# One bank operand for each sum, silu from banks, rounding in two parts, and an own place for the second group's weights

**Chip, cores, metric.** One core of one Trainium2 chip. The metric is the device time of one execution in microseconds (us); medians of several executions are given. TensorE is PE in the profile (its weight loads PEld), VectorE DVE, ScalarE ACT, GpSimd POOL. All runs compared here are of the fast state (e7, run once, has none).

## What is computed

```python
def _attn_ref(x, filt_r, filt_i):                 # x: 8 x 3008 x 256, float32
    X = np.fft.rfft(x, axis=1)
    Y = X * (filt_r + 1j * filt_i)[None, :, :]
    return np.fft.irfft(Y, n=x.shape[1], axis=1).astype(np.float32)

def _moe_ref(x, w_gate, w_val, w_out):            # x: 24064 x 256; weights float64, hidden width 1536
    g = x @ w_gate
    silu = g * (1.0 / (1.0 + np.exp(-g)))
    return (silu * (x @ w_val) @ w_out).astype(np.float32)
```

A filter along the sequence by Fourier transform, then a SwiGLU block over all 24064 tokens.

## The kernel before

The program is 96 steps: 8 batches, each of 4 chunks of tokens times 3 groups of hidden units. A bank is a tile in PSUM, the memory in which PE's products land; most other tiles lie in SBUF. In a step PE makes 26 products of polynomial parts: P and Q (into the four banks k0 to k3, "wk" in the profile), A and B (banks "wa") and E (banks "we"), four matmul records each; it projects the previous step's hidden tile (W1 to W7, banks "wA", "wF", "wG", twelve records each) and does pieces of the next batch's transforms (t0 to t4; "pa", "pb", "pc", "pd"). One string sets the order in which all engines' instructions are issued, and every engine works through its own in that order:

```python
SCHEDULE = """
Q0 n1' h0' Q1 S21' f0 P3 o3' f1 t4.3' t0.0 f3 P1 x0' t0.1 P0 x1' Q2 d1 x2' c0 W1 S00' x3' c1 f2
... (cut) ...
W7 t3.1 E23 o7 W2 e01 l23 g1 t3.2 E01 o2 W5 t3.3 l01 h1 t4.0 B12 o5 t4.1 W4 S01 u12 g0 W3 S11 t4.2
o4
""".split()
BY_POOL = ("01", "12", "13", "23")
```

A token with a prime belongs to the step before. The sums between the products, before the change:

```python
elif kind == "f":   # ACT: bank -> SBUF
    pin(act.mul(self.small(...), t[f"k{i}"], -1.0))
elif kind == "c":   # ACT: bank -> its place in the hidden tile h, in SBUF
    pin(act.copy(out=self.place(i, i), in_=t[f"k{i}"]))
elif kind == "s":   # DVE: two SBUF operands -> bank of A, B
    pin(add(v, self.bank(f"a{at}"), t[f"q{i}"], t[f"p{j}"]))
elif kind == "y":   # GpSimd: two SBUF operands, for four of six pairs
    if at in BY_POOL:
        pin(add(nc.gpsimd, self.small(f"y{at}", 3), self.place(i, i), self.place(j, j)))
elif kind == "e":   # bank of E: by ACT from y, or by DVE from two SBUF operands
    ...
elif kind == "l":   # DVE
    pin(sub(v, self.place(j, i), t[f"e{at}"], t[f"m{at}"]))
elif kind == "g":   # ACT: silu of half a hidden tile, 1504 columns
    pin(act.activation(out=h[:, 4:8], in_=h[:, 4:8], func=AF.Silu))
elif kind == "h":   # DVE: its product, 1504 columns
    pin(v.tensor_tensor(out=h[:, 0:4], in0=h[:, 0:4], in1=h[:, 4:8], op=ALU.mult))
elif kind == "S":   # GpSimd: eight sums of h for the projection
    pin(f(nc.gpsimd, h[:, dst], h[:, a], h[:, b]))
```

`combine_sequence` (token n) makes the sums of the transformed data ("y_t") for a new chunk, by DVE before the change. The float64 weights are rounded to float32 on the chip in 36 half tiles (`round_half`, token "r" in a table by step), before step 0 and in steps 0 to 3 of batch 0; the rounded weights of the three groups then take turns in one place.

Of the kernel before, what the change touches and what calls it, by code (L numbers as in the profile page):

```python
# [53 lines left out]
N1, N2 = 47, 64  # L54
# [27 lines left out]

SCHEDULE = """
Q0 n1' h0' Q1 S21' f0 P3 o3' f1 t4.3' t0.0 f3 P1 x0' t0.1 P0 x1' Q2 d1 x2' c0 W1 S00' x3' c1 f2
t0.2 x4' s01 S10' Q3 s13 x5' o1 c3 A01 A13 m01 t1.0 S31' m13 s03 S20' s23 P2 y13 t1.1 B01 t0.3 d2
A03 u01 A23 c2 t1.2 m03 s02 B13 m23 y12 W6 u13 y23 A02 t2.0 e13 o6 e03 m02 S30' E13 t2.1 t1.3 B03
l13 B23 u03 s12 E03 e12 y01 u23 B02 e02 l03 A12 u02 n3 t2.2 E12 m12 E02 t2.3 l12 e23 t3.0 l02 n2
W7 t3.1 E23 o7 W2 e01 l23 g1 t3.2 E01 o2 W5 t3.3 l01 h1 t4.0 B12 o5 t4.1 W4 S01 u12 g0 W3 S11 t4.2
o4
""".split()  # L90
KS = (-1, 0, 1, 2)
BLOCKS = (0, 1, 3, 2)
PAIRS = ((0, 1), (1, 2), (2, 3), (0, 2), (1, 3), (0, 3))
BY_POOL = ("01", "12", "13", "23")
ORDER = [t for t in SCHEDULE if t[0] in "PQABE"]
SLOT = {p: i for i, p in enumerate(ORDER)}
# [38 lines left out]
def kernel(  # L135
# [23 lines left out]
    t2pool = pool("t2", 2)  # L159
    fpool = pool("fp", 2)  # L160
    tbpool = pool("tb", 3)
    apool = pool("ap", 2)
    bpool = pool("bp", 1)
    gpool = pool("gp", 2)
    t4pool = pool("t4", 2)
    ypool = pool("yp", 2)
    dpool = pool("dram", 2, DRAM)
# [8 lines left out]
    wt_f = wt_t.rearrange("p s z f -> p s (z f)")  # L176
    y_t = cpool.tile([128, 3 * len(PAIRS), TQ], FP32)
    w_dram = wdpool.tile([NG, 128, NPR, 2, 128], FP32, name="w_all")
# [59 lines left out]
    START = 6  # L238
    halves = iter(range(len(weights)))

    def load_weights(i, queue=nc.sync, hold=False):
        if i < len(weights):
            p = spool0 if 2 <= i < 4 else rpool
            raws[i] = p.tile([128, 2, 128, 2], U32, name=f"raw_{i}", tag="raw", bufs=2)
            ins = queue.dma_start(out=raws[i], in_=weights[i][0])
            if hold:
                tc.keep_in_program_order(ins)

    def round_next():


        i = next(halves)
        raw, (use, *at) = raws.pop(i), weights[i][1]
        low, high = raw[:, :, :, 0], raw[:, :, :, 1]
        pw = rpool.tile([128, 2, 128], U32, name=f"pw_{i}", tag="pw")
        w = rpool.tile([128, 2, 128], FP32, name=f"w_{i}", tag="w")
# [4 lines left out]

        pin(v.tensor_scalar(out=man, in0=high, scalar1=0xFFFFF, scalar2=None,
                            op0=ALU.bitwise_and))
        pin(nc.scalar.activation(out=w, in_=man, func=AF.Copy, scale=2.0 ** -20, bias=1.0))
        pin(v.tensor_scalar(out=pw, in0=high, scalar1=20, scalar2=0x7FF,
                            op0=ALU.logical_shift_right, op1=ALU.bitwise_and))
        pin(nc.scalar.activation(out=pw, in_=pw, func=AF.Relu, bias=off_t))
        if i + 1 >= START:

            load_weights(i + 1, nc.scalar, True)  # L270
        v.tensor_scalar(out=pw, in0=pw, scalar1=255.0, scalar2=2.0 ** 23,
                        op0=ALU.min, op1=ALU.mult)
        v.scalar_tensor_tensor(out=pw.rearrange(flat), in0=raw.rearrange(flat2)[:, :, 1],
                               scalar=0x80000000, in1=pw.rearrange(flat),
                               op0=ALU.bitwise_and, op1=ALU.bitwise_or)
        v.scalar_tensor_tensor(out=w.rearrange(flat), in0=raw.rearrange(flat2)[:, :, 0],
                               scalar=2.0 ** -52, in1=w.rearrange(flat),
                               op0=ALU.mult, op1=ALU.add)
        e = nc.gpsimd
        pf = pw.bitcast(FP32)  # L280
        if use == "proj":
            j, l = at
            dst = wo_t[:, j]
            pin(e.tensor_tensor(out=dst[:, ts(l, 2), :], in0=w, in1=pf, op=ALU.mult))
            if l:
                b11, b12, b21, b22, t1, t2, t4 = [dst[:, i] for i in range(7)]
                sub(e, t1, b12, b11)
                sub(e, t2, b22, t1)
                sub(e, b12, b22, b12)
                sub(e, t4, b21, t2)  # L290
            return
        _, i, z = at
        x, y, u = w[:, 0], wt_t[:, SLOT[f"Q{i}"], z], wt_t[:, SLOT[f"P{i}"], z]
        pin(e.tensor_tensor(out=y, in0=w[:, 1], in1=pf[:, 1], op=ALU.mult))
        e.tensor_tensor(out=x if KS[i] else u, in0=x, in1=pf[:, 0], op=ALU.mult)
        if KS[i] == -1:
            sub(e, u, x, y)
        elif KS[i]:
            add(e, u, x, y)
            if KS[i] == 2:  # L300
                add(e, u, u, y)

    def combine_weights(i, j):

        d = j - i
        m = wt_f[:, SLOT[f"A{i}{j}"]]
        ui, uj, yi, yj = [wt_f[:, SLOT[f"{p}{q}"]] for p in "PQ" for q in (i, j)]
        if d == 1:
            negated_sum(m, ui, uj)
        else:  # L310
            add(nc.vector, m, ui, uj)
            nc.vector.tensor_scalar(out=m, in0=m, scalar1=-1.0 / d, scalar2=None, op0=ALU.mult)
        sub(nc.vector, wt_f[:, SLOT[f"B{i}{j}"]], yi, m)
        add(nc.gpsimd, wt_f[:, SLOT[f"E{i}{j}"]], yj, m)

    def keep_weights(g, piece):

        a, b = PIECES[piece]
        nc.sync.dma_start(out=w_dram[g, :, a:b], in_=wt_t[:, a:b])
# [7 lines left out]
    hid = {t: "r" for t in ("P0", "Q2", "W1", "Q3", "A01", "A13", "P2", "B01")}  # L327
    hid |= {f"E{i}{j}": [(i, j)] for i, j in ((0, 2), (1, 3), (0, 3), (0, 1), (2, 3))}
    hid["B12"] = [(1, 2), 0, 1, 2, 3]
    few = {t: "r" for t in ("Q0", "Q1", "P3", "P1")}  # L330
    PREPARE = {0: hid | {t: "r" for t in ("A03", "A23", "A02", "B03")}, 1: hid, 2: few, 3: few}
# [17 lines left out]
    class Spectral:  # L349


        def __init__(self, b):
            self.b = b
            self.d1 = dpool.tile([2 * NS, N2, C], FP32, name=f"d1_{b}", tag="d1")
            self.d2 = dpool.tile([2 * NS, N2, C], FP32, name=f"d2_{b}", tag="d2")
# [25 lines left out]
        def load_two(self, u):  # L381
            if u < N_TWO:
                b = self.b
                if b:
                    self.tb[u] = tbpool.tile([128, NV, 2, 128], FP32, name=f"tb_{b}_{u}", tag="tb")
                    self.load(out=self.tb[u], in_=de_dram[:, ts(u, NV)])

                    f = fpool.tile([128, 2, NV, C], FP32, name=f"f_{b}_{u}", tag="f")
# [5 lines left out]
                p2 = spool0 if b == 0 and u % 2 else t2pool  # L394
                self.t2[u] = p2.tile([128, NV, C], FP32, name=f"t2_{b}_{u}", tag="t2", bufs=2)
# [32 lines left out]
        def stage1(self, u):  # L428

            if self.b:  # L430
                for v in (0, 1, 2) if u == 0 else (u + 2,):
                    self.load_x(v)
# [4 lines left out]
                                         start=True, stop=True))  # L437
            yield
# [5 lines left out]
        def stage2a(self, u):  # L444
# [7 lines left out]
            if self.b:  # L452
                ppool, qpool = apool, bpool
            else:
                ppool = apool if u % 3 == 2 else spool0
                qpool = bpool if u % 2 else spool0
            for i in range(NV):
                self.pinned(nc.tensor.matmul(out=ps[:, i, :], lhsT=self.tb[u][:, i, 0, :],  # L458
                                             rhs=t2[:, i, :], start=True, stop=True))
            pt = ppool.tile([128, NV, C], FP32, name=f"p_{self.b}_{u}", tag="p",  # L460
                            bufs=4 if ppool is spool0 else 2)
            qt = qpool.tile([128, NV, C], FP32, name=f"q_{self.b}_{u}", tag="q", bufs=1)
# [18 lines left out]
        def stage2b(self, u):  # L481
# [6 lines left out]
            p3 = spool0 if self.b == 0 and u % 2 else gpool  # L488
            g = p3.tile([128, NV, C], FP32, name=f"g_{self.b}_{u}", tag="g", bufs=2)
# [42 lines left out]
    def combine_sequence(y, d):  # L532

        v = nc.vector
# [9 lines left out]
        for dst, src, f in ((pe, yb[:, 0:n], -d), (pb, yb[:, d:4], d)):  # L544
            pin(v.scalar_tensor_tensor(out=dst, in0=src, scalar=float(f), in1=pa,
                                       op0=ALU.mult, op1=ALU.add))
# [3 lines left out]
    class Group:  # L550


        def __init__(self, b, k, g, y, following):
            self.b, self.k, self.g, self.y, self.following = b, k, g, y, following
            self.name = f"{b}_{k}_{g}"
            self.tiles = {}
# [4 lines left out]
        def place(self, i, t):  # L561
            at = ((0, 1), (3, 2))[i % 2][t // 2]
            return self.hs[i // 2].rearrange("p (z e) n -> p z e n", z=2)[:, :, at, ts(t % 2, TQ)]

        def small(self, key, bufs):
            t = npool.tile([128, 2, TQ], FP32, name=f"{key}_{self.name}",
                           tag=key if bufs == 1 else key[0], bufs=bufs)
            self.tiles[key] = t
            return t
# [7 lines left out]
        def product(self, p, key, start):  # L577
# [5 lines left out]
            for z in range(2):  # L583
                pin(nc.tensor.matmul(out=ps[:, z], lhsT=wt_t[:, SLOT[p], z], rhs=rhs,  # L584
                                     start=start and z == 0, stop=True, skip_group_check=True))

        def step(self, op):
# [3 lines left out]
            t, v, act = self.tiles, nc.vector, nc.scalar  # L591
            if kind in "PQ":
# [4 lines left out]
            elif kind == "f":  # L597
                pin(act.mul(self.small(f"{'p' if i == 3 else 'q'}{i}", 1), t[f"k{i}"], -1.0))  # L598
            elif kind == "d":
                pin(negated_sum(self.small(f"p{i}", 1), t[f"k{i}"], t[f"q{i}"]))  # L600
            elif kind == "c":
                pin(act.copy(out=self.place(i, i), in_=t[f"k{i}"]))  # L602
            elif kind == "s":
                pin(add(v, self.bank(f"a{at}"), t[f"q{i}"], t[f"p{j}"]))
            elif kind in "AB":
                self.product(op, f"a{at}", False)
            elif kind == "m":
                pin(act.copy(out=self.small(f"m{at}", 5), in_=t[f"a{at}"]))  # L608
            elif kind == "u":
                pin(act.copy(out=self.place(i, j), in_=t[f"a{at}"]))  # L610
            elif kind == "y":
                if at in BY_POOL:
# [231 lines left out]
```

## Time and profile before

| | before |
|---|---|
| time, median of 3 (range) | 3233.56 us (3229.16 to 3238.31) |
| profiled execution | 3229.1 us |
| mean granted clock of PE | 0.969 |
| startup to step 0 | 111.5 us |
| steps 0 to 3 of batch 0 (weights are rounded) | 230.6 us |
| rest of batch 0 | 252.2 us |
| batches 1 to 6 | 2277.6 us |
| batch 7, and the end | 357.2 us |

Read it so: the stretches are differences of step starts; how these are found, the prediction says. 119 us of the 230.6 in the first four steps are standstill or half clock (three steps of 30.3 us, and 21 for step 0, which has no output products yet, would be 112), against some 20 us in each later batch.

### The profile page before, as it was taken

The page shows a single profiled execution, that of the slowest core. Times are in us where ns is not written, and L with a number is a line of the kernel's source. Part 1 is how long each engine was busy: PE and PEld are TensorE (multiplying, and loading weights), DVE is VectorE, ACT ScalarE, POOL GpSimd, SP SyncE. Part 2 cuts the span into 40 slices and gives each one's busy share as a digit, 9 for nine tenths or more (in the row PEclk, how much of TensorE's full clock was granted, in tenths as well). Part 3 has the DMA queues.
Part 4 walks back from the last instruction along what each step waited for, and adds up shares of the span by engine and source line. Part 5 has one row for each costly group of instructions (what it writes and reads, how often), then busy time and mean ns, then how long its engine had stood idle before and what let it go on. Part 6 is the DMA issues. An engine that isn't in the chain of part 4 may idle for free.

```text
span 3229.1 us, 54700 instructions
## 1 busy us (share of the span) xinstructions
PE 2994.4 (93%) x20124; PEld 2849.8 (88%) x20124; DVE 2223.4 (69%) x3198; ACT 1568.9 (49%) x3002; POOL 1558.8 (48%) x1586
## 2 busy tenths in 40 slices
PE   5448999999999999999999999999999999999997
PEld 2347999999998999999999999989989999999997
DVE  5467677667765687656776677766876567767775
ACT  1144544555454544455445555545444554455553
POOL 2255555435454464445453454534544454545555
PEclk9678999999999999999999999999999999999999
DMA  8434656456555565456554566556655555544442
GB/s 228 129 110 161 203 170 185 152 186 208 176 162 163 189 211 167 143 181 197 175 185 156 186 193 191 167 158 193 212 170 158 183 185 187 181 147 143 143 132 68
DMA packets 210483, 551.57 MB, mean 171 GB/s; under 512 B 32502, under 2 KB 105462, under 8 KB 209362
## 3 DMA queue, kind: packets, MB, share of 16 engines
q1 hardware_dynamic: 151116, 462.59, 45.4%
q10 hardware_dynamic: 48864, 57.69, 6.3%
q0 software_dynamic: 10240, 27.80, 2.6%
q8 instruction: 162, 2.65, 0.3%
q14 instruction: 101, 0.83, 0.1%
HBM read 462.76 MB, written 85.20 MB: 170 GB/s over the span
## 4 chain that ended last, share of the span: by engine, by line
PE 79%; DVE 11%; DMA 5%; issue 2%; POOL 2%; ACT 1%; SPq 1%; ACTq 0%; POOLq 0%; DVEq 0%
PE wa L584 22%; PE wA L657 13%; PE wk L584 11%; PE we L584 11%; PE wG L657 7%; DVE wa L199 5%; PE wF L657 4%; PE pd L506 3%; PE pa L436 3%; PE pc L486 2%; PE pb L458 2%; DMA x<-in_x_dram 1%; DMA f<-in_filt_r_dram 1%; DVE h L628 1%; DMA wt_t<-w_all 1%
## 5 line engine op out<-in xcount | busy, mean ns | idle before, releaser
L584 PE MATMUL wa<-y_t,wt_t 128*128 128x188 f32 x4608 | 858.7, 329 | 111.1 <-DVE wa L199 84.1
L584 PEld LDWEIGHTS wa<-y_t,wt_t 128*128 128x128 f32 x4608 | 757.5, 193 | 144.7 <-issue 72.5
L199 POOL TENSOR_TENSOR h<-h 128x376 f32<-128x376 f32 x192 | 190.9, 994 | 1017.6 <-DVE h L628 1017.1
L202 POOL TENSOR_TENSOR h<-h 128x376 f32<-128x376 f32 x576 | 614.5, 1086 | 13.8
L584 PE MATMUL wk<-y,wt_t 128*128 128x188 f32 x3072 | 573.2, 331 | 31.7 <-ACT q L598 21.6
L199 DVE TENSOR_TENSOR wa<-q,p 128x376 f32<-128x376 f32 x576 | 581.7, 1042 | 11.9
L657 PE MATMUL wA<-wo_t,h 128*128 128x128 f32 x4608 | 580.7, 276 | 5.3 <-DVE h L628 3.4
L657 PEld LDWEIGHTS wA<-wo_t,h 128*128 128x128 f32 x4608 | 564.8, 192 | 20.2 <-issue 13.2
L584 PEld LDWEIGHTS wk<-y,wt_t 128*128 128x128 f32 x3072 | 510.5, 196 | 69.8 <-ACT q L598 27.8
L202 DVE TENSOR_TENSOR h<-we,m 128x376 f32<-128x376 f32 x576 | 315.1, 548 | 303.1 <-PE we L584 298.9
L610 ACT COPY h<-wa 128x376 f32<-128x376 f32 x576 | 274.3, 477 | 374.6 <-PE wa L584 353.5
L584 PE MATMUL we<-y_t,wt_t 128*128 128x188 f32 x2304 | 450.0, 325 | 3.5 <-ACT we L616 2.6
L584 PEld LDWEIGHTS we<-y_t,wt_t 128*128 128x128 f32 x2304 | 376.1, 192 | 17.7 <-issue 10.9
L628 DVE TENSOR_TENSOR h<-h 128x1504 f32<-128x1504 f32 x192 | 340.9, 1776 | 69.3 <-ACT h L625 52.3
L608 ACT COPY m<-wa 128x376 f32<-128x376 f32 x576 | 269.0, 477 | 177.0 <-PE wa L584 173.3
L625 ACT ACTIVATE h<-h 128x1504 f32<-128x1504 f32 x192 | 279.8, 1458 | 141.0 <-DVE h L202 137.7
L199 POOL TENSOR_TENSOR y<-h,h 128x376 f32<-128x376 f32 x192 | 218.9, 1140 | 236.6 <-ACT h L602 236.5
L199 DVE TENSOR_TENSOR o<-o,wA 128x384 f32<-128x384 f32 x256 | 141.2, 551 | 232.6 <-PE wA L657 230.1
L657 PE MATMUL wG<-wo_t,h 128*128 128x128 f32 x2304 | 288.5, 275 | 0.2 <-DVE o L199 0.2
L657 PEld LDWEIGHTS wG<-wo_t,h 128*128 128x128 f32 x2304 | 277.1, 192 | 0.3 <-issue 0.3
L602 ACT COPY h<-wk 128x376 f32<-128x376 f32 x384 | 176.2, 474 | 200.2 <-PE wk L584 159.5
L199 POOL TENSOR_TENSOR p<-p,q 128x512 f32<-128x512 f32 x96 | 153.2, 1596 | 172.2 <-DVE q L477 152.0
(77 smaller groups left out, 3115.9 us busy)
## 6 DMA issues: line engine op xcount, KB each, us to landing
wt_t<-w_all SPq DMA_DIRECT2D x186, 896.0 KB
wt_t<-w_all SPq DMA_DIRECT2D x186, 768.0 KB
t<-d SPq DMA_DIRECT2D x192, 128.0 KB
d<-g ACTq DMA_DIRECT2D x192, 128.0 KB
t<-d SPq DMA_DIRECT2D x64, 384.0 KB
d<-t ACTq DMA_DIRECT2D x112, 192.0 KB
tb<-de_tbl SPq DMA_DIRECT2D x84, 256.0 KB
f<-in_filt_r_dram SPq DMA_DIRECT2D x336, 64.0 KB
```

The source lines that it names most:

```text
L199: return eng.tensor_tensor(out=dst, in0=a, in1=b, op=ALU.add)
L202: return eng.tensor_tensor(out=dst, in0=a, in1=b, op=ALU.subtract)
L436: self.pinned(nc.tensor.matmul(out=ps[0:NK], lhsT=wf_t, rhs=self.x.pop(u), start=True, stop=True))
L458: self.pinned(nc.tensor.matmul(out=ps[:, i, :], lhsT=self.tb[u][:, i, 0, :], rhs=t2[:, i, :], start=True, stop=True))
L506: self.pinned(nc.tensor.matmul(out=psv[:, n, :], lhsT=self.t4[k, i][:, n, ts(cb, 128)], rhs=wi_t, start=True, stop=True))
L584: pin(nc.tensor.matmul(out=ps[:, z], lhsT=wt_t[:, SLOT[p], z], rhs=rhs, start=start and z == 0, stop=True, skip_group_check=True))
L602: pin(act.copy(out=self.place(i, i), in_=t[f"k{i}"]))
L608: pin(act.copy(out=self.small(f"m{at}", 5), in_=t[f"a{at}"]))
L610: pin(act.copy(out=self.place(i, j), in_=t[f"a{at}"]))
L625: pin(act.activation(out=h[:, 4:8], in_=h[:, 4:8], func=AF.Silu))
L628: pin(v.tensor_tensor(out=h[:, 0:4], in0=h[:, 0:4], in1=h[:, 4:8], op=ALU.mult))
L657: pin(nc.tensor.matmul(out=self.tiles[at][:, t, :], lhsT=self.hs[i][:, HID[p], t0:t0 + 128], rhs=wo_t[:, JB * q + i, WO[p], :], start=star ...
```

## The change

Its intent, as its code shows it: DVE's sums take one operand from the bank instead of two from SBUF; silu and its product read banks directly, in 16 pieces of 188 columns; the sums over the sequence go to GpSimd (with ACT's multiplications); rounding a half tile is cut in two, and the first part of half i+1 is issued before the second of half i; the second group's weights get a place of their own in step 1 ("lent", later used for transform buffers); x of the next batch is loaded two steps early; and the order is new throughout. The core of the diff (cut: the buffers, the loads, the tables):

```diff
 SCHEDULE = """
-Q0 n1' h0' Q1 S21' f0 P3 o3' f1 t4.3' t0.0 f3 P1 x0' ...
+P3 x1.o' h23' g03' v12' Q0 x2.o' h03' Q2 x3.o' f0 x4.o' t0.0 x03 f2 x5.o' S01' x23 Q1 t0.1 P0 f1
+P2 S00' c0 W1 s13 g0 t0.2 D01 c2 S11' y02 g2 h0 P1 o1 S10' Q3 c1 y01 A13 g1 x01 g3 S21' h1 e01
+t1.0 y12 m13 s01 E01 S20' t1.1 A01 D02 W6 m01 t1.2 D12 l01 B13 u01 o6 B01 v01 g13 W7 S31' h13 g01
+... (cut) ...
+            elif kind == "D":
+                pin(sub(nc.gpsimd, self.small(f"D{at}", "D", 2), t[f"f{i}"], t[f"f{j}"]))
+            elif kind == "x" or kind == "s" and at not in VIA_SBUF[0]:
+                dst = self.small(f"x{at}", "x", 3) if kind == "x" else self.bank(f"a{at}")
+                pin(v.scalar_tensor_tensor(
+                    out=dst, in0=t[f"k{j}"], scalar=-1.0, in1=t[f"f{i}" if j == 3 else f"D{at}"],
+                    op0=ALU.mult, op1=ALU.add))
             elif kind == "s":
-                pin(add(v, self.bank(f"a{at}"), t[f"q{i}"], t[f"p{j}"]))
+                pin(act.copy(out=self.bank(f"a{at}"), in_=t[f"x{at}"]))
+            elif kind == "y" or kind == "e" and at not in VIA_SBUF[1]:
+                dst = self.small(f"y{at}", "y", 2) if kind == "y" else self.bank(f"e{at}")
+                pin(negated_sum(dst, t[f"k{j}"], t[f"c{i}"]))
+            elif kind == "e":
+                pin(act.copy(out=self.bank(f"e{at}"), in_=t[f"y{at}"]))
             elif kind == "l":
-                pin(sub(v, self.place(j, i), t[f"e{at}"], t[f"m{at}"]))
+                pin(sub(v, t[f"e{at}"], t[f"e{at}"], t[f"m{at}"]))
+            elif kind in "gu":
+                ps = t[f"k{i}" if diagonal else f"{'a' if kind == 'g' else 'e'}{at}"]
+                pin(act.activation(out=self.small(op, "g", 3, 1)[:, 0], in_=ps[:, 1], func=AF.Silu))
+            elif kind in "hv":
+                ...
+                pin(v.tensor_tensor(out=dst, in0=ps[:, 0], in1=g, op=ALU.mult))
     def combine_sequence(y, d):
-        v = nc.vector
+        v = nc.gpsimd
         ...
-            pin(v.scalar_tensor_tensor(out=dst, in0=src, scalar=float(f), in1=pa,
-                                       op0=ALU.mult, op1=ALU.add))
+            pin(nc.scalar.mul(dst, src, float(f)))
+            pin(add(v, dst, dst, pa))
+    def weights_of(b, k, g):
+        return wt_1 if (b, k, g) == (0, 0, 1) else wt_t
+        for h in halves[i:i + 1] + (halves[i - 1:i] if i else []):
+            next(h, None)
+                if b + 2 < B and (step, op) == (9, "B01"):
+                    for u in range(3):
+                        following.load_x(u)
```

## The prediction

> **What bounds the kernel now.** I read the page's busy shares first, then the table of stretches, the timeline around one stall, and the waits.
>
> ```profile
> PE 2994.4 (93%) x20124; PEld 2849.8 (88%) x20124; DVE 2223.4 (69%) x3198; ACT 1568.9 (49%) x3002; POOL 1558.8 (48%) x1586
> ...
> PEclk9678999999999999999999999999999999999999
> ```
>
> PE is busy nearly all the time; the rest have room on average. So gain can only come from the stretches where PE stands still. The program is 96 steps (8 batches x 4 chunks x 3 weight groups), each opening with the four banks wk, 32 matmul records; counting those in the timeline gives the step starts, from which I cut the stretches. Columns: busy us of PE, PEld, DVE, ACT, POOL, then granted clock, DMA share, GB/s.
>
> ```profile
> 111.50:200.10 88.60, 36.52 (x128) 29.29 (x128) 55.45 (x135) 26.26 (x61) 36.31 (x64) 0.61 0.40 134
> 200.10:261.50 61.40, 38.32 (x212) 34.13 (x211) 43.41 (x81) 27.21 (x56) 32.07 (x45) 0.78 0.40 134
> 261.50:301.00 39.50, 33.16 (x200) 30.27 (x199) 27.60 (x51) 19.76 (x40) 19.56 (x24) 0.91 0.48 151
> ...
> 1042.80:1073.10 30.30, 30.30 (x201) 27.75 (x200) 19.09 (x32) 16.74 (x32) 12.55 (x13) 1.00 0.66 205
> 1196.80:1233.30 36.50, 32.53 (x227) 31.98 (x226) 25.72 (x28) 18.12 (x34) 16.77 (x20) 0.95 0.46 152
> 1263.50:1298.10 34.60, 32.24 (x211) 30.78 (x210) 26.48 (x38) 15.42 (x29) 16.49 (x17) 0.95 0.56 178
> ```
>
> The first three are steps 0 to 2 of batch 0; step 3 takes 41.1 us. The last three are steps 2, 7 and 9 of batch 2. Step 2 is what a step without a stall looks like. In the chain a product (4 records) takes 0.64 us, an output product (12 records) 1.34, a spectral piece 0.86: 26 x 0.64 + 7 x 1.34 + 5 x 0.86 = 30.3 us, just the 30.30 seen. Batch 2's twelve steps take 38.3, 31.4, 30.2, 30.2, 31.2, 31.4, 31.0, 36.5, 30.3, 34.6, 29.6, 27.7; the same sum for their own pieces is 358, so the batch loses 24 us, mostly in steps 0, 7 and 9. Batches 1 to 6 all repeat this (18 to 24 us lost). A stall in step 7 of batch 5, on DVE, PE and POOL:
>
> ```profile
> 2346.66 5.54 DVE L199 TENSOR_TENSOR wa<-q,p 128x376 f32<-128x376 f32 x1
> ...
> 2352.35 0.88 PE L584 MATMUL wa<-y_t,wt_t 128*128 128x188 f32 x4 [2.52 <-DVE wa L199]
> ...
> 2348.01 0.98 POOL L199 TENSOR_TENSOR y<-h,h 128x376 f32<-128x376 f32 x1
> 2348.95 0.97 POOL L199 TENSOR_TENSOR y<-h 128x376 f32<-128x376 f32 x1
> 2349.89 0.96 POOL L202 TENSOR_TENSOR h<-h 128x376 f32<-128x376 f32 x1
> 2350.82 0.96 POOL L199 TENSOR_TENSOR y<-h 128x376 f32<-128x376 f32 x1
> ```
>
> One DVE sum of two SBUF tiles takes 5.54 us, and ends just after POOL's run of back-to-back adds; PE waits 2.5 us for it, and the clock falls after (0.95 over the step). That is no accident of one step (min/median/max ns):
>
> ```profile
> L199 DVE TENSOR_TENSOR wa<-q,p x576: 542/842/5546, 151.9 to 3189.8; 128x376 f32<-128x376 f32 x192
> ```
>
> The waits from step 4 on (total us, times, longest):
>
> ```profile
> PE wa L584 <- DVE wa L199: 39.2, 37, 2.5
> ...
> ACT h L602 <- DVE p L206: 34.8, 51, 2.2
> ...
> PE pa L436 <- DMA x<-in_x_dram: 25.7, 6, 5.0
> ```
>
> At its shortest the sum takes 0.54, on average 1.04 (582 us / 576): 0.5 x 576 = 288 us of DVE's 2223 are waiting inside the instruction. The last line is step 0's stall: the next batch's first x load is issued where it is needed.
>
> **What the Trainium skill says.** "SBUF — State Buffer", Who interferes with whom: a DVE instruction with two SBUF inputs contends with a GpSimd instruction that reads SBUF, the later one blocks in full, and one SBUF input does not contend. The trace agrees: 5.54 against 0.54 us, while sums with one bank operand (o with wA) keep to 0.54 to 0.56. "PSUM — Partial Sum Buffer", PSUM bank collisions raise a hardware error: two engines may not touch a bank at once, reads included. The program orders them: ACT's copy of wk waits for DVE's read of wk (34.8 us above) though it needs nothing from it. This matters for the change, whose banks have more readers. "TensorE: Matmul & The Clock Gate", Part 1: an idle window of some 3.4 us halves the clock; the 0.61 and 0.95 above agree, so a stall costs more than itself. "ScalarE: Activation LUTs", What ACT_TABLE_LOAD costs: 186 + 0.833 N ns for an activation with constants, 499 at 376 elements; the trace has 485 to 495.
>
> **The change part by part.**
> 1. Sums. Every steady DVE sum now has one bank operand (k) and one SBUF operand (f, c or a difference D made by POOL). Per step DVE has 12 such sums, 6 subtractions in place, and 16 products of half width instead of two of 1504 columns (1.78 us each). Durations: 0.55 for 376 columns; the slope from 376 (0.548) to 512 (0.685) is 1 ns a column, so 0.36 for 188. 18 x 0.55 + 16 x 0.36 + output sums 3.1 + spectral 2.3 (both unchanged: their rows over 96) = 21 us a step, against 23 now. The sums over the sequence (1.9 us a step) move to POOL.
> 2. ACT: 16 silus of 188 columns (0.477 less 188 x 0.8 ns = 0.33) instead of two of 1.46; 6 sums and e banks arrive by ACT copies from SBUF; fewer f and c copies: 5.3 + 2.9 (m) + 2.9 (f, c) + 3.0 + 0.6 + 1.9 + 0.6 = 17 us, as now.
> 3. POOL: 8 sums of h (0.98 each unblocked) + 3 D + 3.1 for the sequence + 2.3 = 16.2 us, as now. Nothing passes 21 of 30 us, so PE stays the bound: matmuls are the same in number and size.
> 4. What PE waits for in a steady step. I laid the new order of PE out at the paces above and put the chains beside it. The tightest: P1 ends at 6.66 us of the step; copy c1 (starts 0.2 later, 0.48), sum y01 (0.55), silu g1 (0.33), g3 (0.2 more), copy e01 (0.49) give 9.0 for E01, due at 8.8; A01 comes 0.35 late. The other sums have 0.5 to 3 us of slack, and at most 7 of 7 banks are held (around 23.5 us). I take 0.5 us lost a step, 6 a batch.
> 5. x of the next batch is asked for two steps ahead: step 0's 4 to 5 us go (within the 6 above).
> 6. Rounding. 36 half tiles at 2.05 us of DVE each (0.46 + 0.38 + 0.29 + 0.42 + 0.49). Now in-place weights of the next group wait for PE's last use, and each half crosses DVE, ACT, DVE in turn. In the new kernel the second group has its own place and DVE starts half i+1 before ending half i. DVE then sets step 0: 12 x 2.05 + 6 pairs x 1.7 + 15.5 for the step's own = 50; with waits for the raw loads 60. Step 1: 8 x 2.05 + 10 + 22 = 49, say 51. Steps 2 and 3: four halves ahead of the first sum, 8 us less some 4 of slack, 35 each. Startup to step 0: five halves move ahead of it, mostly under the reload of the transformed data: 112, unchanged.
>
> **Sum.** Startup 112; steps 0 to 3: 60 + 51 + 35 + 35 = 181 (231 now); rest of batch 0: 238 + 5 = 243 (252 now); batches 1 to 6: 6 x (358 + 6) = 2184 (2278 now); batch 7 and end 350 (357 now): 3070, and 4 for time over span: 3074 us, 4.9% faster.
>
> **Rivals.** (a) A new wait takes the old one's place: banks live longer (k3 from 0 to 21 us of a step) and pass DVE, ACT, DVE in turn, and POOL's D is now in the chain, so every step may lose 1.5 us instead of 0.5: +90, 3165. For: more crossings of 0.05 to 0.2 us each; against: slack counted above. (b) Rounding in steps 0 and 1 is bound by raw loads and by the two-input instructions it still has, not by order: nothing gained there, +50, 3124. The chain shows raw loads of 3 to 7 us in step 0, which speaks for it. (c) PE loses almost nothing after step 3 (as in steps 2 and 8 now, 0.1 us): -37, and some faster start: 3030. (d) DVE becomes the bound: its 34 sums and products would each have to be 0.25 us longer than estimated to make 21 into 29.5 us a step; the measured 0.55 of such sums speaks against it, and the time would then be as in (a).
>
> **Range and chances.** (c) is the low end, 3030; half of (a) with part of (b) the high end, 3135. Slower than 3169 (2%) needs (a) in full and more. Faster 0.94, same 0.05, slower 0.01.
>
> **What would show it.** Right: no DVE instruction of the steady part over 0.8 us; DVE busy about 2100; the wait of PE for DVE sums gone; no pa wait for x; steps of 30.2 to 31; batches 1 to 6 near 364 us each; granted clock over 0.98; step 0 near 60. Wrong: step lengths of 32 with PE waiting for ACT copies or for banks, or first steps as long as now.

## The result, and the profile after

The changed kernel takes 3138.43 us (median of 4 runs, 3135.62 to 3141.20), the kernel before in the same job 3234.50: ratio 0.9704, 95% interval 0.9687 to 0.9721, 3.0% faster. (A ratio here is the mean time of one kernel's fast runs over that of the other's of the same rounds, so not quite the ratio of the medians quoted.) The direction was predicted; the time lies 64 us above the predicted one and 3 above the range.

The page's lines of the kernel after, to be held against those of before that the prediction shows:

```profile
PE 2989.7 (95%) x20124; PEld 2831.6 (90%) x20124; DVE 1974.2 (63%) x4446; ACT 1513.4 (48%) x3898; POOL 1585.3 (50%) x1778
...
PEclk9778999999999999999999999999999999999998
```

DVE has 1248 instructions more and 249 us less busy time. The same stretches of the kernel after (steps 0 to 3 of batch 0, then steps 2, 7 and 9 of batch 2; columns as in the prediction):

```profile
115.10:181.20 66.10, 34.57 (x128) 30.47 (x128) 40.67 (x113) 24.69 (x59) 36.86 (x53) 0.68 0.49 168
181.20:235.20 54.00, 39.87 (x212) 36.64 (x211) 42.08 (x103) 24.32 (x63) 29.29 (x46) 0.81 0.26 81
235.20:275.40 40.20, 33.81 (x200) 30.70 (x199) 23.05 (x60) 19.20 (x50) 21.99 (x28) 0.87 0.64 218
275.40:313.70 38.30, 32.89 (x200) 29.78 (x199) 25.53 (x60) 17.89 (x48) 21.38 (x30) 0.91 0.41 132
989.90:1020.60 30.70, 30.70 (x200) 27.69 (x199) 17.80 (x42) 16.05 (x42) 15.81 (x16) 1.00 0.63 201
1145.00:1175.90 30.90, 30.72 (x226) 30.30 (x225) 19.12 (x44) 16.08 (x42) 14.11 (x17) 1.00 0.52 167
1206.90:1239.20 32.30, 31.17 (x210) 29.61 (x209) 23.22 (x50) 14.17 (x37) 18.04 (x20) 1.00 0.64 198
```

Step 7 has gone from 36.5 to 30.9 us at a full clock, and the first four steps from 88.6, 61.4, 39.5 and 41.0 to 66.1, 54.0, 40.2 and 38.3. Two of DVE's groups of sums in the kernel after (min/median/max ns, first and last start):

```profile
L218 DVE SCALAR_TENSOR_TENSOR y<-wk,c x288: 532/549/552, 138.7 to 3088.8; 128x376 f32<-128x376 f32 x144
...
L625 DVE SCALAR_TENSOR_TENSOR x<-wk,f x192: 540/549/552, 121.3 to 3083.2; 128x376 f32<-128x376 f32 x192
```

Where the sum of before ran from 542 to 5546 ns, these never pass 552. Of PE's own waits, from step 4 to the last step (total us, times, longest), these are the two largest; five more rows add up to 2.5 us. The waits for DVE's sums into banks and for x are gone:

```profile
PE we L603 <- ACT we L634: 20.1, 38, 1.5
PE wa L603 <- ACT wa L629: 3.0, 4, 1.1
```

Where the 90 us came from, by stretch:

| us | before | predicted | after |
|---|---|---|---|
| startup to step 0 | 111.5 | 112 | 115.1 |
| steps 0 to 3 | 230.6 | 181 | 198.6 |
| rest of batch 0 | 252.2 | 243 | 246.5 |
| batches 1 to 6 | 2277.6 | 2184 | 2212.7 |
| batch 7 and the end | 357.2 | 350 | 366.5 |
| span | 3229.1 | 3070 | 3139.4 |

And the mean length of each step over batches 1 to 6 (the last row is an experiment below):

| step | 0 | 1 | 2 | 3 | 4 | 5 | 6 | 7 | 8 | 9 | 10 | 11 |
|---|---|---|---|---|---|---|---|---|---|---|---|---|
| before | 36.98 | 31.39 | 30.24 | 30.24 | 31.13 | 31.30 | 30.96 | 35.21 | 30.25 | 34.44 | 29.73 | 27.72 |
| after | 30.68 | 30.64 | 30.61 | 30.61 | 30.71 | 31.67 | 30.97 | 30.97 | 30.96 | 31.81 | 31.09 | 28.08 |
| e10_two_sbuf | 30.95 | 30.91 | 30.88 | 30.88 | 35.64 | 32.05 | 32.25 | 35.40 | 32.13 | 32.29 | 36.36 | 28.43 |

Of the 65 us won in batches 1 to 6, step 0 gave 38 and steps 7 and 9 gave 41, while the other nine steps lost 14.

### The profile page after: what moved, and what is told of

It reads as the page before. It is cut to its first block, busy times and chain, and to the rows that moved or that the text cites. A ratio compares the mean times of both kernels' runs of the same rounds, so it can differ in the third digit from the quotient of the medians.

```text
span 3139.4 us, 57065 instructions
## 1 busy us (share of the span) xinstructions
PE 2989.7 (95%) x20124; PEld 2831.6 (90%) x20124; DVE 1974.2 (63%) x4446; ACT 1513.4 (48%) x3898; POOL 1585.3 (50%) x1778
## 4 chain that ended last, share of the span: by engine, by line
PE 80%; ACT 5%; DVE 3%; POOL 2%; issue 1%; DMA 1%; ACTq 1%; POOLq 0%; DVEq 0%
PE wa L603 21%; PE wA L679 14%; PE wk L603 13%; PE we L603 11%; PE wG L679 8%; PE wF L679 4%; PE pd L525 3%; PE pa L453 3%; PE pc L504 2%; PE pb L479 2%; DVE y L218 1%; ACT g L645 1%; ACT c L622 1%; ACTq L513 1%; DMA out_dram<-o 1%
## 5 line engine op out<-in xcount | busy, mean ns | idle before, releaser
L214 POOL TENSOR_TENSOR h<-h 128x376 f32<-128x376 f32 x576 | 552.5, 984 | 0.0
L214 DVE TENSOR_TENSOR we<-we,m 128x376 f32<-128x376 f32 x576 | 311.3, 556 | 375.8 <-ACT m L638 177.1
L211 POOL TENSOR_TENSOR h<-h 128x376 f32<-128x376 f32 x192 | 185.0, 987 | 430.2 <-DVE h L650 429.7
L645 ACT ACTIVATE g<-wa 128x188 f32<-128x188 f32 x576 | 188.6, 328 | 425.6 <-PE wa L603 267.4
L214 POOL TENSOR_TENSOR D<-f,f 128x376 f32<-128x376 f32 x288 | 280.3, 987 | 72.2 <-ACT f L618 72.1
L645 ACT ACTIVATE u<-we 128x188 f32<-128x188 f32 x576 | 185.0, 326 | 247.6 <-DVE we L214 239.2
L211 POOL TENSOR_TENSOR lent<-lent 128x512 f32<-128x512 f32 (+2 forms) x94 | 116.2, 1237 | 326.3 <-DVE lent L495 304.8
L668 POOL DMA_DIRECT2D out_dram<-o x192 | 110.8, 582 | 315.5 <-DVE o L211 313.4
L650 DVE TENSOR_TENSOR h<-wa,g 128x188 f32<-128x188 f32 x576 | 201.6, 350 | 83.9 <-ACT g L645 79.0
L650 DVE TENSOR_TENSOR h<-we,u 128x188 f32<-128x188 f32 x576 | 201.7, 350 | 78.2 <-ACT u L645 68.3
L218 DVE SCALAR_TENSOR_TENSOR y<-wk,c 128x376 f32<-128x376 f32 x288 | 157.2, 546 | 99.6 <-ACT c L622 98.3
```

What stands on the lines that cost most here:

```text
L211: return eng.tensor_tensor(out=dst, in0=a, in1=b, op=ALU.add)
L214: return eng.tensor_tensor(out=dst, in0=a, in1=b, op=ALU.subtract)
L218: return nc.vector.scalar_tensor_tensor(out=dst, in0=a, scalar=-1.0, in1=b, op0=ALU.mult, op1=ALU.subtract)
L645: pin(act.activation(out=self.small(op, "g", 3, 1)[:, 0], in_=ps[:, 1], func=AF.Silu))
L650: pin(v.tensor_tensor(out=dst, in0=ps[:, 0], in1=g, op=ALU.mult))
L668: pin(nc.gpsimd.dma_start(out=rows[(TOK[t] + skip) // NH:(TOK[t] + 128) // NH, ts(2 * k + i, NH), :], in_=outs[b, k][i][skip:128, t, :]))
```

## The experiments

The theory going in: (1) what steps 7 and 9 gained is the one-bank operand, since a DVE sum of two SBUF operands stands still beside GpSimd; (2) step 0's gain is the early x; (3) the first steps gained by interleaved rounding and by the second group's own place; (4) what the prediction lacks lies in E01's chain and in GpSimd's queue in step 0. The rival: the new order itself does it all. Ratios are set against the kernel before of the same job; the changed kernel's own is 0.9704. Differences in us are between medians of different jobs, in which the kernel before took 3234 to 3238, so a few us of the whole time say nothing by themselves; the step lengths say more.

| run | us | ratio, 95% interval | batches 1 to 6 | steps 0 to 3 |
|---|---|---|---|---|
| changed kernel | 3138.43 | 0.9704 (0.9687 to 0.9721) | 2212.7 | 198.6 |
| e1_w6_first | 3176.24 | 0.9817 (0.9801 to 0.9833) | 2241.8 | 203.1 |
| e2_seq0_dve | 3133.22 | 0.9686 (0.9668 to 0.9703) | 2210.6 | 192.9 |
| e3_seq_dve | 3174.40 | 0.9813 (0.9789 to 0.9837) | 2236.2 | 196.4 |
| e4_x_late | 3195.46 | 0.9879 (0.9863 to 0.9895) | 2268.4 | 198.2 |
| e5_round_whole | 3134.70 | 0.9688 (0.9660 to 0.9717) | 2211.3 | 197.4 |
| e6_before_less_pool | 3232.27 | 0.9994 (0.9969 to 1.0018) | 2280.8 | 225.9 |
| e8_in_place | 3139.40 | 0.9696 (0.9677 to 0.9716) | 2210.1 | 197.6 |
| e10_two_sbuf | 3302.81 | 1.0205 (1.0176 to 1.0234) | 2329.0 | 202.3 |
| e11_proj_early | 3129.66 | 0.9668 (0.9636 to 0.9700) | 2209.6 | 187.2 |
| e12_w6_o6 | 3151.62 | 0.9736 (0.9708 to 0.9765) | 2220.3 | 201.2 |
| e13_best | 3119.22 | 0.9646 (0.9631 to 0.9662) | 2209.1 | 183.3 |

(e7_lock_alone was one look, not timed.)

### Two SBUF operands again, in place (e10_two_sbuf)

Six of the twelve sums of a step have a partner whose copy already lies in SBUF. They read it there instead of in the bank; nothing else changes.

```diff
-  out=dst, in0=t[f"k{j}"], scalar=-1.0, in1=t[f"f{i}" if j == 3 else f"D{at}"],
+  out=dst, in0=t[f"k{j}" if j == 3 else f"c{j}"], scalar=-1.0, in1=...
-  pin(negated_sum(dst, t[f"k{j}"], t[f"c{i}"]))
+  pin(negated_sum(dst, t[f"k{j}" if j == 3 else f"c{j}"], t[f"c{i}"]))
```

> The changed kernel with one thing undone: the six sums whose partner already has a copy in SBUF (01, 02, 12 of each sort) read that copy instead of the bank, so that both operands are in SBUF. Same instructions, same count, same order, same numbers. Theory (an addition by VectorE with two SBUF operands stands still while GpSimd adds, which is why bank operands help): these six groups, now 0.55 us at any time, get a mean of 0.7 to 1.1 us and a longest of over 2 us; TensorE waits more for the sums; batches 1 to 6 take 20 to 60 us more, some 3160 to 3200 in all. Rival (what helps is the new order and the early x; operands do not matter as sums have slack): durations stretch but the time stays within 8 us of 3138.

Measured: 3302.81 us, 2% slower than the kernel before, so the whole gain and more is lost by the operands alone. The same group of sums now, in the same view as above:

```profile
L218 DVE SCALAR_TENSOR_TENSOR y<-c,c x288: 533/1056/7284, 139.5 to 3250.5; 128x376 f32<-128x376 f32 x144
```

One instance in the timeline, step 10 of batch 2, on DVE, POOL and PE:

```profile
1301.24 0.98 POOL L214 TENSOR_TENSOR D<-f,f 128x376 f32<-128x376 f32 x1
1301.76 5.55 DVE L218 SCALAR_TENSOR_TENSOR y<-c,c 128x376 f32<-128x376 f32 x1 [0.40 <-ACT c L622]
1302.18 3.79 POOL L214 TENSOR_TENSOR h<-h 128x376 f32<-128x376 f32 x4
1305.94 0.97 POOL L214 TENSOR_TENSOR D<-f,f 128x376 f32<-128x376 f32 x1
...
1308.59 0.68 PE L603 MATMUL we<-y_t,wt_t 128*128 128x188 f32 x1 [4.25 <-ACT we L635]
```

The same place of the changed kernel:

```profile
1245.50 0.55 DVE L218 SCALAR_TENSOR_TENSOR y<-wk,c 128x376 f32<-128x376 f32 x1 [0.40 <-ACT c L622]
...
1245.93 3.80 POOL L214 TENSOR_TENSOR h<-h 128x376 f32<-128x376 f32 x4
```

The sum with a bank operand takes 0.55 us in the middle of GpSimd's run, the one with two SBUF operands 5.55: it starts during the first of six additions and ends 0.4 us after the last. The product E01 behind it then waits 4.25. Theory 1 holds for step 7, which is back at 35.4 us (the table above; the stall is at E01 now); its size was even underestimated (+116 us in batches 1 to 6 where 20 to 60 were expected), and the rival that operands don't matter falls. Step 9 doesn't come back: 32.3 us here, 31.8 in the changed kernel, 34.4 before. There the sum that PE waited 2.15 us for had begun late, behind over 8 us of DVE work without a pause (sums over the sequence, the product of 1504 columns, the transform); which part of the change removed that is not shown.

### The lock by itself (e7_lock_alone)

Appended to the changed kernel, after all its work: eight DVE sums of two SBUF operands alone, eight beside a run of GpSimd sums, and eight of one bank and one SBUF operand beside such a run.

```diff
+    for n in range(8):                            # alone, then beside the run of GpSimd's
+        pin(add(v, b1, two(0), two(1)))
+    for n in range(12):
+        pin(add(e, dst[2 + n % 2], two(2), two(3)))
+    ...
+    for n in range(8):                            # one operand from a bank
+        pin(add(v, b1, b0, two(1)))
```

> The changed kernel with a measurement of 30 to 40 us after its last step (its time means nothing): eight DVE sums of two SBUF tiles (128x376) into a bank alone; the same eight beside twelve back-to-back adds of POOL; then eight DVE sums of a bank and an SBUF tile beside twelve adds of POOL. Theory of the lock: alone 0.42 to 0.55 us each; beside POOL the two-SBUF sums wait for POOL's whole instruction each time or for the whole run (1 us and more each, one of them perhaps 5 or more); with one bank operand 0.55 us each, as alone. Rival: all three at 0.55.

Measured (timeline of the end):

```profile
3128.47 4.69 DVE L211 TENSOR_TENSOR wmb<-y_t 128x376 f32<-128x376 f32 x8
...
3134.77 14.62 POOL L211 TENSOR_TENSOR lent<-y_t 128x376 f32<-128x376 f32 x13
...
3135.42 9.41 DVE L211 TENSOR_TENSOR wmb<-y_t 128x376 f32<-128x376 f32 x8
...
3150.98 11.26 POOL L211 TENSOR_TENSOR lent<-y_t 128x376 f32<-128x376 f32 x12
3151.52 4.69 DVE L211 TENSOR_TENSOR wmb<-wmb,y_t 128x376 f32<-128x376 f32 x8
```

Alone 4.69 us, beside GpSimd 9.41, and with a bank operand 4.69 again. GpSimd pays too: 14.62 / 13 = 1.12 us for one addition instead of 11.26 / 12 = 0.94. Here the two take turns, at most 1.2 us for a DVE sum. Inside the kernels most of the stretched sums are held up by one or two additions as well; only 6 of 576 in the kernel before (all in step 7) and 25 of the 288 shown of e10 (in steps 4, 7 and 10, and one in step 1) take over 3 us, as they wait for a whole run. What makes it the one or the other isn't settled.

### Less of GpSimd in the kernel before (e6_before_less_pool)

```diff
-BY_POOL = ("01", "12", "13", "23")
+BY_POOL = ()
```

> The kernel before with four sums a step (y) taken from POOL and made by DVE straight into the bank, as it already did for two: POOL has 4.5 us less a step, DVE 4 two-operand sums of 0.55 to 0.65 us more. Theory of the lock: the sums wa get shorter although DVE has more to do, mean from 1.04 to 0.8 us or less and longest from 5.5 to below 4, and the stalls of PE in steps 7 and 9 shrink; time 3180 to 3225. Rival (DVE's load makes the stalls): the sums keep their mean and the time rises above 3240.

Measured: no difference, where 3180 to 3225 us was expected. The longest sum fell from 5.5 to 3.6 us as expected, but the mean only from 1.04 to 0.975, for GpSimd's eight sums of h a step stay (six of them 1.13 us on average), and DVE got the four differences of two SBUF operands in return. Step 7 won 2.9 us (35.21 to 32.33), steps 5 and 9 lost 1.7 and 1.0. This run didn't remove the cause and tells nothing against it; it shows that taking a quarter of GpSimd's busy time away (1559 to 1168 us) was not enough.

### Sums over the sequence on DVE (e3_seq_dve, e2_seq0_dve)

All of them, or only those of the very first chunk, go back to DVE with two SBUF operands.

```diff
-    def combine_sequence(y, d):
-        v = nc.gpsimd
+    def combine_sequence(y, d, on_dve=True):      # e2: False, and True in the one call ahead of step 0
+        v = nc.vector if on_dve else nc.gpsimd
 ... (cut: where on_dve, a multiplication and its sum are one DVE instruction again)
```

> The changed kernel with all sums over the sequence (nine instructions in three steps, both operands in SBUF) back on DVE. Theory of the lock: beside POOL's runs of adds these DVE instructions take far longer than alone (0.55 to 1.3 us for 376 to 564 columns where POOL is idle; up to several us, mean above 1.5 times that), and what DVE holds up behind them gives PE stalls of over 1 us again in steps 0, 3, 6, 9 (after the sums); steps lengthen by 1 to 3 us each, 20 to 60 us over the whole. Rival (load only: DVE has room for 1.9 us a step more, POOL gets rid of 3.1): the DVE instructions keep their lengths and the time stays within 8 us of 3138.

Measured: 36 us more. In step 6 of batch 2, where the run shows most:

```profile
1136.91 2.22 DVE L211 TENSOR_TENSOR y_t<-y 128x188 f32<-128x188 f32 x1
...
1140.31 1.68 PE L607 MATMUL wa<-y_t,wt_t 128*128 128x188 f32 x8 [1.80 <-DVE wa L629]
```

A sum of 188 columns that takes 0.34 us at its shortest in this run took 2.22, and the sum behind it came 1.8 us late for PE: step 6 is 2.1 us longer on average (33.09 against 30.97), and 12.7 of the 23.5 us of batches 1 to 6 are that step. So moving these sums to GpSimd paid in this order, and the stretched sum says for the same reason.

> The changed kernel, but the first chunk's sums over the sequence, before step 0, are made by DVE as in the kernel before; all later ones stay on POOL. Theory: in step 0 PE's wait of 13.5 us comes from these nine operations on POOL (8.8 us), behind which POOL's products of the weight rounding queue; the rounding's two buffers are not free, and DVE and ACT, in program order, stand behind them. Then this wait falls below 4 us, and the time by about 10 us: 3128. Rival (raw weight loads bound step 0): the wait only moves to the loads and the time stays at 3138 within 3.

Measured: 5 us less, half of what was expected. The intervals of the two ratios overlap, but step 0 shows it: 61.8 us, against 66.0 to 66.1 in the changed kernel, e1, e4, e11 and e12, which leave it alone. PE's wait of 13.5 us there became 8.0 (below 4 was expected), as GpSimd's nine sums no longer stood ahead of the rounding. Startup, 117.0 us, is within the 115.1 to 118.0 of those runs.

### Early x undone (e4_x_late)

```diff
-                if b + 2 < B and (step, op) == (9, "B01"):
-                    for u in range(3):
-                        following.load_x(u)
+            if self.b and u == 0:                 # in stage1, where it is needed
+                for v in range(3):
+                    self.load_x(v)
```

> The changed kernel with the early loads of the next batch's first three x pieces undone: they are issued in stage one of step 0, as in the kernel before. Theory: PE's wait for x of 4 to 5 us returns in step 0 of batches 0 to 6, with about 1.7 us of half clock after it: 7 times 5 to 6.5, so 35 to 45 us more, about 3178, and this is half of what batches 1 to 6 gained. Rival (the loads come early enough either way since SP's queue is no longer held): within 10 us of 3138.

Measured: 57 us more, all of it in step 0 of batches 1 to 6: 40.16 us on average instead of 30.68. The wait of PE, from step 0 of batch 1 on: 

```profile
PE pa L456 <- DMA x<-in_x_dram: 40.7, 6, 6.9
```

6.8 us a batch by itself, and the rest of the 9.5 by the halved clock after it. Why it is longer than in the kernel before (4 to 5 us) was not looked into. Theory 2 holds: this smallest part of the diff is worth 56 us in these batches once the rest is there.

### The two parts for rounding (e5_round_whole, e8_in_place)

```diff
-        for h in halves[i:i + 1] + (halves[i - 1:i] if i else []):
+        for h in halves[i:i + 1] * 2:             # e5: a half is ended before the next is begun
```

> The changed kernel with the rounding in one piece again: both parts of half i follow one another, nothing of half i+1 is between them. Theory of the prediction (the parts interleaved save DVE the way over ACT and back, 0.9 us or more for each of 24 to 28 halves): steps 0 to 3 get 15 to 25 us longer in all, about 3158. Rival (the rounding is held by POOL's products, the raw loads and the place of the calls): within 6 us.

```diff
-        return wt_1 if (b, k, g) == (0, 0, 1) else wt_t
+        return wt_t                               # e8: no own place; each half prepared after
+                                                  # PE's last use of what it overwrites
```

> The changed kernel without the own place for the second group's weights: groups 1 and 2 are both prepared in the place of the group in use, each half and each pair put after the last product that uses the old values (so the preparation starts after Q3 and its pairs end with the step). Theory of the prediction: waiting for the old weights' last use was a large part of the first two steps' cost; step 0 and 1 get 10 to 20 us longer together and step 1 and 2 begin with waits for the last pairs: about 3155. Rival (the order of the queues and the raw loads set these steps, not the place): within 5 us of 3138.

Measured: 3134.70 and 3139.40 us, both within 4 us of the changed kernel. Neither part taken away by itself costs anything, so theory 3 has no support. What made the first four steps 32 us shorter then isn't isolated: the order of the weights and of their sums, three raw buffers instead of two, and the fixed places in each engine's order are left, or each of the two parts makes up for the other. Both at once were not undone.

### Projection weights earlier (e11_proj_early)

In the changed kernel PE's first output product of step 2 waits, and again in step 3 (5.0 us):

```profile
246.57 2.50 PE L679 MATMUL wA<-wo_t,h 128*128 128x128 f32 x10 [6.39 <-POOL wo_t L290]
```

The four halves of these weights are rounded at the head of the very step that needs them. In the experiment a step's worth of room is given:

```diff
-   1: eight | pairs,
-   2: {t: "r" for t in ("P3", "Q1", "P0", "P2")},
-   3: {t: "r" for t in ("P3", "Q1", "P0", "P2")}}
+   1: eight | pairs | {t: "r" for t in ("A01", "E02", "W3", "B23")},
+   2: {t: "r" for t in ("A02", "E03", "W5", "B02")}}
```

> The four halves of the projection weights of group 1 are rounded within step 1, those of group 2 in the later part of step 2, instead of at the head of the step that needs them. Theory (steps 2 and 3 lose their 10 and 8 us since the first output product waits 6.4 and 5.0 us for weights that are rounded just ahead of it): waits of the output product for POOL gone, steps 2 and 3 at 31 to 33 us (from 40.2 and 38.3), step 1 longer by at most 8 us (from 54.0): 8 to 14 us less, about 3128. Rival (VectorE's work in step 1 sets the time, and what steps 2 and 3 gain step 1 loses): within 4 us of 3138.

Measured: 9 us less. Steps 0 to 3 take 66.0, 57.1, 33.5 and 30.6: steps 2 and 3 won 14.4, step 1 lost 3.1. As the theory said.

### E01's chain (e1_w6_first, e12_w6_o6)

In the timeline of step 10 the copy that opens E01's bank comes late, as bank A's copy stands ahead of the chain's own on ACT; PE waits 0.67 us for it (0.27 in step 8, where it is a sum of DVE's that stands ahead):

```profile
1246.31 0.47 ACT L691 COPY o<-wA 128x384 f32<-128x384 f32 x1
1246.67 0.49 ACT L622 COPY c<-wk 128x376 f32<-128x376 f32 x1
...
1248.21 0.49 ACT L634 COPY we<-y 128x376 f32<-128x376 f32 x1
```

Two attempts to put W6 (1.34 us of PE's own work) ahead of E01:

```diff
-t1.0 y12 m13 s01 E01 S20' t1.1 A01 D02 W6 m01 t1.2 D12 l01 B13 u01 o6 B01 v01 g13 W7
+t1.0 y12 m13 s01 W6 E01 S20' t1.1 A01 D02 m01 t1.2 D12 l01 B13 u01 o6 B01 v01 g13 W7   (e1)
+t1.0 y12 m13 s01 W6 E01 S20' t1.1 A01 D02 o6 m01 t1.2 D12 l01 B13 u01 B01 v01 g13 W7   (e12)
```

> The changed kernel with one move in PE's order: W6 (1.34 us of output products) now comes ahead of E01 instead of after A01. Theory: what a steady step still loses (0.5 us in steps without a stall, 1.1 in most of batch 7, 1.7 in step 10) is E01 and A01 coming before their operands, because copy c1, sum y01, silu g1, silu g3 and the copy into the bank of E01 follow one another after P1; with W6 in between the chain is hidden. Then the steps take 30.2 to 30.3 us, batches 1 to 6 about 361 instead of 368.8, batch 7 about 8 us less, the whole about 55 us less: 3083. Rival (banks or the DVE and ACT load are the limit): the wait moves to B13 or W7 and the time stays within 10 us of 3138.

Measured: 38 us more. The gaps at E01 and A01 are gone from PE's records, and W7 waits 0.23 to 0.51 us in every step instead: it needs bank A, which o6 reads, and o6 stands behind l01 in DVE's order (in steps 1, 4, 7 and 10 ACT makes o6, behind u01).

> Output product W6 ahead of E01 as in the first experiment, and its sum o6 right behind it in VectorE's order, ahead of l01, so that bank A is free for W7. Theory (the loss of 0.9 us a step is half E01's chain; the first attempt failed since o6 came too late for W7): no waits at E01, A01 and W7, 0.4 us less a step in steps 1 to 11, 25 to 35 us less in all: about 3108. Rival (the order is so full that whatever is moved opens another wait): 3130 to 3175, with the wait at another product.

Measured: 13 us more. W7's wait is gone too, and steps 0 to 3 of these batches are shorter than in the changed kernel (30.43 to 30.55). But PE now waits 0.8 to 1.0 us for the copy m01 ahead of B01 in step 10, and W6 itself 0.7 to 0.9 for GpSimd's sums of h in step 6, and steps 6 and 9 to 11 lose more than the rest won. Both times the rival was right: a slot that is full passes the wait on.

### The parts that helped, together (e13_best)

e2 and e11, and the eight sums of h of the very last group on DVE, which has nothing else to do there. In the changed kernel the end of the last step is:

```profile
3111.91 1.85 PE L679 MATMUL wA<-wo_t,h 128*128 128x128 f32 x12 [2.67 <-POOL h L214]
3114.51 2.90 PE L679 MATMUL wA<-wo_t,h 128*128 128x128 f32 x12 [0.74 <-DVE o L211]
```

```diff
+                end = (self.b, self.k, self.g) == (B - 1, NCHUNK - 1, NG - 1)
-                pin(f(nc.gpsimd, h[:, dst], h[:, a], h[:, b]))
+                pin(f(nc.vector if end else nc.gpsimd, h[:, dst], h[:, a], h[:, b]))
```

> The changed kernel with the parts that helped, together: the first chunk's sequence sums on VectorE (5 us by themselves), the projection weights rounded earlier (9 us), and, not tried before, the eight sums of h of the very last group on VectorE instead of GpSimd, as GpSimd sets the end there: TensorE waits 2.7 us for them, and the clock falls to half for the 8 us that follow. Expected: the first two add up in step 0 and steps 2 and 3 (steps 0 to 3 together 182 us, from 198.6), the last step 3 to 7 us shorter (from 58.8), some 3118 us in all. If the gains do not add up (one takes the other's room on VectorE in the first steps): 3128, as the best of them alone.

Measured: 3119.22 us, the fastest kernel of the study, 0.6% below the changed one (0.9646 / 0.9704). Steps 0 to 3 take 183.3 us and the last step 53.8 (58.9 in the changed kernel):

```profile
3093.87 1.60 PE L683 MATMUL wA<-wo_t,h 128*128 128x128 f32 x12 [1.80 <-DVE h L214]
3096.12 1.60 PE L683 MATMUL wA<-wo_t,h 128*128 128x128 f32 x12 [0.65 <-DVE o L211]
```

The wait is 0.9 us shorter, and after it the products keep to 1.60 us instead of 2.9: most of the 5 us is the clock that doesn't fall. That is in part luck of the execution. In e1, where GpSimd still makes these sums, the same wait left the clock whole:

```profile
3150.24 1.60 PE L679 MATMUL wA<-wo_t,h 128*128 128x128 f32 x12 [2.66 <-POOL h L214]
3152.59 1.58 PE L679 MATMUL wA<-wo_t,h 128*128 128x128 f32 x12 [0.74 <-DVE o L211]
```

The last step took 54.6 us there, and 56.1 to 60.4 in the nine other timed runs of the changed order that have this wait. Where the clock holds anyway, the shorter wait, 0.9 us, is what would be left of this gain.

## Why the prediction was right and wrong

The mechanism came true; the sum of the stretches did not. The profiled span is 69 us above the 3070 predicted: 29 in batches 1 to 6, 18 in steps 0 to 3, 16 in batch 7 and the end, and some 3 each in the rest of batch 0 and in the startup (112 predicted, 115.1 here, up to 118.0 in other runs).

**Right: what the sums gain.** No such sum passes 0.56 us, PE's waits for them are gone, step 7 lost its stall and step 9 most of it, the clock rose to 0.982. The mechanism, named from the spread of one instruction's duration, is shown by e10 and e7, though for step 7 and not for step 9, which the prediction put down to it as well. DVE's busy time fell to 1974 us where 2100 was given. (The mean of 1.04 us is the view's; 582 / 576 would be 1.01.)

**Right: early x.** The wait for x is gone and step 0 is 30.7 us. Its weight was not seen: e4 puts it at 57 us of the whole time.

**Wrong in size: batches 1 to 6, 2184 predicted, 2212.7 measured.** Half of these 29 us is a wrong sum. With the prediction's own lengths, and the pieces that the records of batch 2 count (16 pa, 12 pb, 12 pc and 16 pd, so 56), a batch without loss is 12 x (26 x 0.64 + 7 x 1.34) + 56 x 0.86 = 360 us, not 358. The other half is "I take 0.5 us lost a step": against 360 the 368.8 us of a batch are 0.7 lost a step. By the usual length of each kind of record, steps 0 to 4 and 11 lose 0.3 to 0.4 us, nearly all at E01 and A01, where the prediction had its tightest chain; 6 to 8 lose 0.6 to 0.7, and 5, 9 and 10 lose 1.4 to 1.6, since there work of DVE and ACT for the second transform (and o1) stands ahead of links of the chains. In step 9 of batch 2, for one, ACT issues two transfers of the transform (2.04 us) just ahead of a silu and a bank copy, and PE waits 0.94 us for that copy. The prediction laid the chains beside a step whose engines were free to answer at once. e1 and e12 show that moving one product's place doesn't take the loss away. (The 0.9 us a step in e12's expectation rests on the 358.)

**Wrong in size: steps 0 to 3, 181 predicted (60 + 51 + 35 + 35), 198.6 measured (66.1, 54.0, 40.2, 38.3).** Two things were left out. In step 0, GpSimd has three sums for E's weights and the nine sums over the sequence ahead of its part of the rounding; there are only two buffers for that, so DVE and ACT, in their fixed order, stand still behind it, and PE behind them:

```profile
117.16 5.24 POOL L211 TENSOR_TENSOR wt_t<-wt_t 128x256 f32<-128x256 f32 x3 [1.90 <-DVE wt_t L330]
122.36 0.97 POOL L211 TENSOR_TENSOR y_t<-y 128x376 f32<-128x376 f32 x1
...
132.55 0.29 DVE L268 TENSOR_SCALAR w<-raw 128x256 uint32<-128x256 uint32 x1 [10.24 <-POOL lent L211]
...
136.37 2.87 PE L603 MATMUL wk<-y,wt_t 128*128 128x188 f32 x8 [13.51 <-ACT f L618]
```

The prediction had counted the sums' 1.9 us a step as moved to an engine with room, and not asked what stands behind them in that engine's order at the one place where it has none. e2 shows 5.7 us of it in these steps. And in steps 2 and 3 the projection weights come too late, as e11 shows (11.4 us in these steps). With both put right the stretch is 183.3 us (e13), near the 181 predicted. Its reasons for the gain here, interleaving and the own place, found no support in e5 and e8, although the gain itself (32 us) came; what brought it stays open.

**Wrong in size: batch 7 and the end, 350 predicted, 366.5 measured.** Eight of batch 7's first eleven steps have no transform piece between E01's chain and E01, and PE waits 0.8 to 0.9 us there (1.5 in step 10); steps 1, 4 and 7, which have pieces, don't wait. And GpSimd's eight sums in a row at the end cost a wait of 2.67 us and some 8 us of products at half clock; e13 wins 5 us of it, in part by luck.

**Read too far: the clock.** The prediction found the page's idle window of some 3.4 us in agreement with the 0.95 of step 7, but PE's longest wait for a sum was 2.5 us (see the closing list).

**The rivals.** (a), a new wait in the old one's place, was what happened, at a fifth of its size in steady steps (0.2 us a step more than predicted, not 1.0). (b), nothing gained in steps 0 and 1, did not hold: 30 of the 39 us came. (c) held for no step, and (d) did not occur: DVE is busy 63%.

Undone one at a time in the changed kernel, one-bank operands, early x and GpSimd's sums are worth 116, 56 and 24 us of batches 1 to 6, 196 together, while the whole change gave 65. That is no contradiction if the new order has so little slack that each delay reaches PE, where the order of before hid most of them. One estimate speaks for it: count times mean less the unblocked mean, DVE's sums stand still for some 283 us in e10 and 287 in the kernel before. It was not tested; nor were the order itself, or silu and product in pieces from banks, ever undone alone. The worth of a part holds only for the order that it stands in.

## What to carry to other kernels

Where DVE and GpSimd work at the same time, look at the spread of one instruction's duration before its mean: a sum that took ten times its shortest time (5.5 against 0.54 us) stood still inside the instruction, where the views of waits don't count it; an operand taken from a bank removed it at no cost in the sum's own length (4.69 us for eight). When work is moved to an engine with room on average, ask what stands behind it in that engine's order at its busiest place. Lay chains of a new order against the fullest steps and those with least filler, not the typical one.

## What the Trainium skill lacked or had wrong

- "SBUF — State Buffer", Who interferes with whom: its rule on two SBUF inputs beside GpSimd agrees in full (eight sums: 4.69 us alone, 9.41 beside GpSimd, 4.69 with one bank operand). It speaks of one instruction that blocks another, and leaves open what comes of runs of them: a DVE sum waited for six GpSimd additions in a row (5.55 us) in e10, and took turns with them (1.2 us each) in e7.
- "TensorE: Matmul & The Clock Gate", Part 1, gives one idle window of some 3.4 us as what halves the clock. Here shorter waits did it, though not each time. The wait of 2.67 us at the end was followed by half clock in nine of ten timed runs (products of 2.9 us instead of 1.5 in the changed kernel; not in e1), and five of six waits of 2.15 us in step 9 of the kernel before were followed by 3.41 us at half clock. After the wait of 1.80 us in e13 the products stayed at 1.6. So waits shorter than the page's window matter, and what the same wait costs differs from run to run.
